# Batched VectorE exponentials and norm transposes by DMA in a one-core attention block

## The chip, the cores and the metric

The kernel runs on one core of a Trainium2 chip. The metric is the device time of one execution in microseconds, the median of several. A profile shows the span of one execution, which is some 2 us shorter than its time. Engines are named as in the profile: PE (matmul), PEld (weight load), DVE (VectorE), ACT (ScalarE), POOL (GpSimd), SP (SyncE). SP issues the DMAs.

## The reference

The block is a layer norm, an attention with 32 heads of 20 columns, and a gated product without activation, both with residuals, over 2048 tokens of 640 columns in bf16.

```python
def _A_ref(x, wqkv, wo):                       # B, S, D, H = 1, 2048, 640, 32; Dh = 20
    q, k, v = split(x @ wqkv)
    scores = einsum("bhqd,bhkd->bhqk", q, k) * Dh ** -0.5
    p = softmax(scores)
    return merge(einsum("bhqk,bhkd->bhqd", p, v)) @ wo

def _B_ref(x, w_gate, w_up, w_down):           # F = 1728
    return ((x @ w_gate) * (x @ w_up)) @ w_down

h  = x + _A_ref(layernorm(x), A_wqkv, A_wo)
h2 = h + _B_ref(layernorm(h), B_w_gate, B_w_up, B_w_down)
```

## The kernel before

The 2048 x 2048 scores of 32 heads need 134 million exponentials. They are handed out as 2048 PSUM banks of 128 x 512; four banks, one for each head of a group of four, make a slot. 313 of the banks go to VectorE, which makes the exponential from integer arithmetic, the rest to ScalarE. The queries are processed in six passes (512, 512, 384, 256, 256, 128 wide). The second stage (output projection, norm, gate, up, down) of a pass lies beside the attention of the next; the last one's is the tail.

The order of the instructions on each engine is fixed when the program is built: a list scheduler with a rough model of durations takes, on each engine and on the DMA queue, the ready task of the lowest priority number, and writes it down. On the chip each engine then runs its list in that order.

```python
def pick(self, eng):
    ...
    start = max(self.free[eng], best_r)
    ...
    t = min((t for r, t in ready if r <= start), key=lambda t: (t.prio, t.seq))
    return start, t
```

VectorE's exponentials take one pass per bank to add a bias, and then four passes over a pair of banks:

```python
def tail(self):                                # when two banks are collected
    ...
    def p2():
        nc.vector.tensor_scalar(f[:, 0:n, :], it[:, 0:n, :], 127, None, ALU.bitwise_and)
    def p3():
        nc.vector.tensor_scalar(h[:, 0:n, :], f[:, 0:n, :], QR, QK, ALU.subtract, ALU.mult)
    def p4():
        nc.vector.tensor_tensor(fb[:, 0:n, :], h[:, 0:n, :], f[:, 0:n, :], ALU.mult)
    def p5():
        nc.vector.tensor_tensor(e16[:, 0:n, :], it[:, 0:n, :], fb[:, 0:n, :], ALU.add)
    ...
```

The layer norm's rows are turned by PE in column tiles, and a copy takes them out of PSUM:

```python
def transpose_group(src, ev, dst, done, eng, prio, tag):
    def step(c):
        def fn(ps, first, last):
            pt = ps.bitcast(BF16)
            for i in range(4):
                nc.tensor.transpose(pt[32 * i:32 * i + 32, c * P:(c + 1) * P],
                                    src[:, c * P + 32 * i:c * P + 32 * i + 32], ident[:])
        return fn
    ...
```

All DMAs share SP's one queue.

The softmax here doesn't subtract the row's maximum and nothing guards it: scores larger than these inputs give would overflow.

## Time and profile before

| | before |
|---|---|
| time, median of 3 | 885.79 us (883.98 to 886.77) |
| span of the profiled run | 883.0 us |
| first exponential on ScalarE starts | 17.70 us |
| its last exponential ends | 834.8 us |
| tail: from there to the end | 48.2 us |
| ScalarE in exponentials (page) | 795.4 us in 758 instructions |
| ScalarE idle ahead of exponentials in between | 19.8 us: 14.3 before 210 us, 0.9 to 780, 4.6 after |
| VectorE busy | 754.5 us, 85% |

Read it as a sum along ScalarE: start, exponentials, idle, its few copies with the waits around them and the idle times too short for a bracket, tail: 17.7 + 795.4 + 19.8 + 1.9 + 48.2 = 883.0. The prediction's idle of 21.1 is counted by stretches and contains copies; the 19.8 here are the idle times that the timeline puts ahead of exponentials.

### The profile page before, as it was taken

How to read it: one execution, taken by the hardware profiler on the slowest of the kernel's cores; microseconds unless marked ns; L12 is line 12 of the kernel's file. 1: busy time of each engine (PE TensorE's matmuls, PEld its weight loads, DVE VectorE, ACT ScalarE, POOL GpSimd, SP SyncE). 2: the span in 40 equal slices, each digit the busy share in tenths (PEclk: the TensorE clock that was granted, in tenths of full speed). 3: DMA queues.
4: the chain of work that ended last, by engine and by line, in shares of the span. 5: the costliest groups of instructions: out<-in, count | busy, mean ns of one | idle time of the engine just before them, and what ended most of it. 6: DMA issues, size and time to landing. Idle time of an engine off the chain costs nothing. (4 is left out here: it accounts for less than half of the span.)

```text
span 883.0 us, 36981 instructions
## 1 busy us (share of the span) xinstructions
PE 832.6 (94%) x16596; PEld 367.6 (42%) x16596; DVE 754.5 (85%) x1608; ACT 804.4 (91%) x780; POOL 20.8 (2%) x32
## 2 busy tenths in 40 slices
PE   6999999999999999999999999999999999999995
PEld 2444342232334322222344433344444445565774
DVE  4654886999899999999999999989989997998652
ACT  3699989999999999999999999999999999998801
POOL 2020000000000000000000000000000000000000
PEclk9999999999999999999999999999999999999999
DMA  6131212212230233211310233161034311274100
GB/s 206 39 102 29 82 56 63 84 40 79 64 89 22 67 96 90 53 41 36 67 38 28 50 79 72 27 146 34 23 90 97 66 26 31 67 154 77 23 16 19
DMA packets 132950, 56.62 MB, mean 64 GB/s; under 512 B 103096, under 2 KB 130744, under 8 KB 132792
## 3 DMA queue, kind: packets, MB, share of 16 engines
q1 hardware_dynamic: 132792, 54.27, 24.5%
q8 instruction: 129, 2.11, 1.0%
q14 instruction: 29, 0.24, 0.1%
HBM read 45.89 MB, written 8.09 MB: 61 GB/s over the span
## 5 line engine op out<-in xcount | busy, mean ns | idle before, releaser
L740 ACT ACTIVATE E<-A 128x1536 bf16<-128x1536 f32 (+1 forms) x758 | 795.4, 1183 | 21.1 <-PE A L429 12.4
L429 PE MATMUL A<-qT,kT 32*128 32x256 bf16 (+3 forms) x3024 | 296.9, 299 | 22.8 <-ACT E L740 18.6
L429 PEld LDWEIGHTS <-kT 32*128 32x128 bf16 (+1 forms) x3768 | 101.5, 92 | 256.6 <-issue 216.0
L429 PE MATMUL acc<-E,Vx 128*32 128x256 bf16 (+3 forms) x2808 | 190.1, 304 | 4.7 <-ACT E L740 3.0
L754 DVE TENSOR_SCALAR i<-m 128x512 int16<-128x512 f32 x185 | 125.9, 684 | 11.8 <-PE m L429 10.5
L429 PEld LDWEIGHTS <-Vx 128*32 128x32 bf16 x3328 | 69.5, 95 | 102.5 <-issue 94.0
L784 DVE TENSOR_TENSOR fr<-hl,fr 128x1024 bf16<-128x1024 bf16 x157 | 107.0, 682 | 2.0
L787 DVE TENSOR_TENSOR ED<-i,fr 128x1024 int16<-128x1024 int16 x157 | 106.4, 678 | 1.3
L754 DVE TENSOR_SCALAR i<-A 128x512 int16<-128x512 f32 x128 | 87.7, 685 | 11.4 <-PE A L429 9.5
L429 PE MATMUL m<-lnT,Wr 128*32 128x512 bf16 (+7 forms) x1200 | 74.9, 347 | 2.2 <-DVE lnT L1016 0.8
L429 PE MATMUL m<-qT,kT 32*128 32x256 bf16 (+3 forms) x304 | 71.6, 297 | 0.0
L429 PE MATMUL m<-Wd,hh 128*32 128x320 bf16 (+1 forms) x1456 | 71.0, 301 | 0.2 <-DVE i L754 0.2
L429 PE MATMUL m<-ln2T,wg 128*32 128x512 bf16 (+2 forms) x980 | 70.0, 348 | 0.8 <-DVE i L754 0.8
L429 PE MATMUL m<-ln2T,wu 128*32 128x512 bf16 (+2 forms) x980 | 68.7, 348 | 1.3 <-DVE i L754 1.3
L429 PE MATMUL acc<-zt 128*32 128x512 bf16 (+3 forms) x992 | 67.2, 341 | 0.0
L781 DVE TENSOR_SCALAR hl<-fr 128x1024 bf16<-128x1024 int16 x157 | 65.4, 417 | 1.5
L778 DVE TENSOR_SCALAR fr<-i 128x1024 int16<-128x1024 int16 x157 | 64.4, 414 | 1.3
L429 PEld LDWEIGHTS <-hh 128*32 128x32 bf16 (+1 forms) x1792 | 42.9, 96 | 25.8 <-issue 16.4
L429 PE MATMUL m<-shared,On 128*32 128x320 bf16 x1024 | 49.0, 301 | 0.1
L1406 DVE TENSOR_TENSOR hh<-gs,m 128x512 bf16<-128x512 bf16 (+3 forms) x66 | 36.0, 545 | 9.4 <-PE m L429 5.0
L1395 DVE CAST gs<-m 128x512 bf16<-128x512 f32 (+5 forms) x62 | 35.1, 567 | 7.0 <-PE m L429 6.3
L429 PEld LDWEIGHTS <-Wr 128*32 128x32 bf16 (+1 forms) x1200 | 27.6, 96 | 27.2 <-issue 18.1
(71 smaller groups left out, 541.4 us busy)
## 6 DMA issues: line engine op xcount, KB each, us to landing
wg<-in_B_w_gate_dram SPq DMA_DIRECT2D x47, 160.0 KB
wu<-in_B_w_up_dram SPq DMA_DIRECT2D x47, 160.0 KB
rb<-rd SPq DMA_DIRECT2D x16, 256.0 KB
kT<-kq SPq DMA_DIRECT2D x24, 128.0 KB
kq<-stg SPq DMA_DIRECT2D x24, 120.0 KB
out_dram<-ot SPq DMA_DIRECT2D x16, 160.0 KB
shared<-in_A_x_dram SPq DMA_DIRECT2D x14, 160.0 KB
Wd<-in_B_w_down_dram SPq DMA_DIRECT2D x13, 160.0 KB
```

The costliest lines, as they stand in the source:

```text
L429: nc.tensor.matmul(out_, lhsT=lhsT, rhs=rhs, start=start, stop=stop)
L740: apart(readers, nc.scalar.activation(E[:, 0:size, :], src[:, 0:size, :], ACT.Exp, scale=LN2_ / UNIT))
L754: apart(readers, nc.vector.tensor_scalar(it[:, pos, :], bank.ap, BIAS, 0.0, ALU.add, ALU.max))
L778: nc.vector.tensor_scalar(f[:, 0:n, :], it[:, 0:n, :], 127, None, ALU.bitwise_and)
L781: nc.vector.tensor_scalar(h[:, 0:n, :], f[:, 0:n, :], QR, QK, ALU.subtract, ALU.mult)
L784: nc.vector.tensor_tensor(fb[:, 0:n, :], h[:, 0:n, :], f[:, 0:n, :], ALU.mult)
L787: nc.vector.tensor_tensor(e16[:, 0:n, :], it[:, 0:n, :], fb[:, 0:n, :], ALU.add)
L1395: r = en.add("DVE", dve_ns(w), [e, was], lambda: nc.vector.tensor_copy(gs[0:M, 0:w], ps[0:M, 0:w]), 1)
L1406: r = en.add("DVE", dve_ns(w), [e, ce, was], lambda: nc.vector.tensor_tensor(hh[0:M, 0:w], gs[0:M, 0:w], ps[0:M, 0:w], ALU.mult), 1)
```

## The change

It does four things. VectorE's batch becomes a whole slot of four banks. Layer norm rows are turned by DMA transposes instead of PE: all of the second stage, and tokens 1024 to 2047 of the first (`TURN = 2` of four chunks). In the tail, when the attention is done, matmuls use the full width of PE, and the last two head groups of the last pass and the last one of the pass before get their softmax sums by a small matmul instead of a round trip of three DMAs. The first weights that are loaded serve two head groups, and priorities and spreading of the second stage are set per pass. Two smaller settings change with these: VectorE may take banks from bank 96 on, and a limit at bank 1800 replaces a limit on the second stage's lateness (`LAG`).

```diff
+QK0 = 2 * HP * DH + PADR
+TURN = 2
+FAST_LAST = 2
+FAST_PREV = 1
+LNP = (1.2, 1.2, 1.2, 1.2, 0, 0)
+WP = (1, 1, 1, 1, 0, 0)
...
-SPREAD = 1.2
+SPREAD = (1.0, 1.0, 0.9, 0.8)
-LAG = 100
+M_END = 1800
...
-    I16t = tiles(keep, NI16, [P, 2, QW], I16, "i16_")
-    FR = tiles(keep, 2, [P, 2, QW], I16, "fr")
-    HL = tiles(keep, 1, [P, 2, QW], BF16, "hl")
-    ED = tiles(keep, NED, [P, 2, QW], I16, "ED")
+    DT = tiles(keep, ND, [P, HP, QW], I16, "D")
+    FR = keep.tile([P, HP, QW], I16, name="fr")
+    HL = keep.tile([P, HP, QW], BF16, name="hl")
...
     def columns(ps, lhsT, rhs, start, stop, n, width=P):
+        if pe.mode == "F":
+            mm(ps[0:width, 0:n], lhsT[:, 0:width], rhs, start, stop)
+            return
...
+        if g >= G - FAST.get(p, 0):
+            spread(p, g, free, a, b, spots)
+            return free
...
+    def turn_rows(src, dst, deps, prio):
+        return dma(lambda: nc.sync.dma_start_transpose(dst, src), deps, prio=prio, size=2 * P * D * 2)
...
+            if ch >= TURN:
+                lnT_ev[tt] = turn_rows(outs[i], lnT[:, :, tt * P:(tt + 1) * P], [evs[i]], 0)
+                ln_free[i] = lnT_ev[tt]
+                continue
...
-                g = transpose_group(l2[i % 2], e, ln2T[:, :, i * P:(i + 1) * P], done, "DVE", 1, f"t{p}{i}")
+                lev[i] = turn_rows(l2[i % 2][:], ln2T[:, :, i * P:(i + 1) * P], [e, fr.get("ln2T")], 0.5)
...
-D_START = 2 * HP * NT
+D_START = 96
```

## The prediction

> **What bounds the kernel now.** I read the page of the kernel before, then the busy time of each engine by stretches, then ScalarE in order of time, then the chain of work that ended last. The stretches cut the 883.0 us span into a start, the attention proper and a tail. Columns: stretch, length, then busy us (instruction count) of PE, weight load, VectorE, ScalarE, GpSimd, then granted clock, DMA share, GB/s.
>
> ```profile
> 1.70:17.70 16.00, 12.05 (x164) 5.24 (x165) 10.02 (x35) 3.84 (x7) 5.14 (x11) 1.00 0.96 284
> 17.70:34.70 17.00, 15.34 (x288) 7.03 (x291) 6.18 (x18) 8.57 (x9) 1.01 (x1) 1.00 0.16 47
> 34.70:57.40 22.70, 22.25 (x388) 8.50 (x384) 16.54 (x51) 22.11 (x24) 6.27 (x3) 1.00 0.16 46
> 57.40:89.10 31.70, 31.34 (x702) 14.18 (x694) 13.07 (x32) 29.48 (x32) 0.11 (x1) 1.00 0.24 60
> 89.10:200.00 110.90, 104.97 (x1537) 37.22 (x1535) 96.46 (x187) 106.93 (x101) 0.00 (x0) 1.00 0.22 66
> 200.00:800.00 600.00, 577.26 (x11035) 243.38 (x11035) 564.19 (x1160) 596.47 (x565) 5.94 (x7) 1.00 0.27 64
> 800.00:836.00 36.00, 33.41 (x1136) 22.26 (x1133) 28.01 (x73) 32.42 (x30) 0.70 (x1) 1.00 0.25 48
> 836.00:883.00 47.00, 36.03 (x1376) 29.82 (x1364) 20.04 (x57) 3.72 (x14) 0.55 (x1) 0.98 0.06 17
> ```
>
> From 200 to 800 us ScalarE is idle for 3.5 us of 600: it is the bound there. VectorE is at 94% and PE at 96%, but PE's share contains matmuls of zeros (acc<-zt and m<-zt) that only fill waits, so PE has room. ScalarE's first exponential starts at 17.70 and its last ends at 834.8. Between them it idles 11.2 us up to 89.1 (71.4 minus 8.57, 22.11 and 29.48), 4.0 up to 200, 3.5 up to 800 and 2.4 after: 21.1 us in all. Then follow 1.2 us to the last attention matmul at 836.0, and a tail of 47.0 us without exponentials, which hangs on PE: over 5% of the span. So the time is: start 17.7 + exponentials 795.4 (page) + ScalarE's idle and one copy 21.7 + 48.2. VectorE's busy time is in no term of it.
>
> The tail must be read in the chain that ended last (start, us, what). Its second half is:
>
> ```profile
> 864.40 0.40 PE b L429 x14
> 864.80 0.56 PE m L429 x40
> 865.36 1.01 PE b L429 x74
> 866.37 1.51 issue
> 867.87 0.85 PE b L429 x46
> 868.72 0.28 PE m L429 x20
> 869.00 0.28 PE b L429 x20
> 869.28 0.28 PE m L429 x20
> 869.56 0.29 PE b L429 x22
> 869.84 1.51 issue
> ```
>
> PE runs 14+40+74 = 128 matmuls, waits 1.51 us for nothing that the profile shows, runs 46+20+20+20+22 = 128, and waits 1.51 us again. A matmul and its weight load are two instructions, so the pause comes every 256. The page gives 129 instruction packets of 2.11 MB, 16.4 KB each. I take the pauses for PE waiting for its instructions: 128 pairs last 1.83 us there, so one block takes some 3.34 us to arrive (my estimate, the sum of both).
>
> **What the Trainium skill says.** "Runtime: NRT & Kernel Launch", section "Instruction fetch mechanics", says that instructions come in blocks of 16 KiB, 256 each, the refill mostly hidden. Size and period agree with this trace; "hidden" does not hold in the tail. "TensorE: Matmul & The Clock Gate", section "Back-to-back issue gap", gives about 81 ns per matmul for streams of load and matmul with 128 columns. Here 20 column-tiled matmuls, five full-width steps, take 0.28 us, 56 ns a step; no full-width step can be read in this trace, so it stays open which holds after the change. "VectorE: DVE Perf Modes", section "The perf-mode tier table", has bf16 tensor_scalar at four elements a cycle and tensor_tensor at two, 693 and 1224 ns for 2048. The trace has 418 and 683 ns for 1024, whose slopes lead to about those figures. "DMA: Bandwidth & Descriptors", section "DMA Transpose (X-bar)", tells only that the crossbar does transposes issued from SP or ACT for 2-byte types; no run here shows the duration yet.
>
> **The change part by part.**
>
> *Exponentials on VectorE.* Four rows of the groups view carry this (count | busy us, mean ns | idle):
>
> ```profile
> L784 DVE TENSOR_TENSOR fr<-hl,fr 128x1024 bf16<-128x1024 bf16 x156 | 106.6, 683 | 2.0
> L787 DVE TENSOR_TENSOR ED<-i,fr 128x1024 int16<-128x1024 int16 x156 | 106.0, 679 | 1.2
> L781 DVE TENSOR_SCALAR hl<-fr 128x1024 bf16<-128x1024 int16 x156 | 65.1, 418 | 1.5
> L778 DVE TENSOR_SCALAR fr<-i 128x1024 int16<-128x1024 int16 x156 | 64.1, 415 | 1.3
> ```
>
> A pair of banks costs 2195 ns, two pairs 4390. The forms of 512 columns take 424 and 288 ns, so each further 512 costs 258 and 128; at 2048 I get 1197 and 672 ns, 3738 for the four operations. By the instruction order there are 77 such batches and 3 of three banks instead of 156 pairs and one single: VectorE saves about 47 us. But banks on VectorE only rise from 313 to 317 of 2048, since the share of 0.17 stays. ScalarE goes from 539 two-bank and 219 three-bank exponentials to 528 and 225. In the saturated stretch 32 two-bank ones take 29.48 us, 921 ns each; with 424 ns more for a third bank (the means by form are 1485 and 1061 ns) the 758 add to 795.4 at 927 and 1351 ns. The new mix is 528 x 0.927 + 225 x 1.351 = 793.4 us: 2 us saved. The 47 us of VectorE lie beside ScalarE and buy almost nothing. Starting those banks at 96 rather than 256, and taking fewer after 1800, moves them without adding any.
>
> *Transposes by DMA.* 16 of the second stage and 8 of the first leave PE (20 matmuls, about 0.45 us each, 11 us) and VectorE (0.48 us each, 11.6 us). Off the bound again, but in the first stage the keys of tokens 1024 on now wait for four transposes on the one queue. In PE's new order only two units of scores stand before 140 value matmuls, one dense and one direct projection and 16 zero matmuls, some 6 us of PE against 1.9 us of ScalarE: I expect a new ScalarE gap of 4 to 5 us there, more if the transposes are slow.
>
> *The start.* ScalarE lacks work here:
>
> ```profile
> 29.31 0.59 ACT L1154 CAST kT<-m 128x512 bf16<-128x512 f32 x1 [0.73 <-PE m L429]
> 34.72 22.11 ACT L740 ACTIVATE E<-A 128x1024 bf16<-128x1024 f32 x24 [4.83 <-PE A L429]
> ```
>
> Group 1's projections come late behind values and transposes. The change loads 172 weight columns first, enough for both groups, and PE's order now has group 1 before the values. That should remove most of the 8 us idle of 17.7 to 34.7, and start the first exponential about 1 us later (16 more matmuls, four steps at 0.43 us, in part hidden). With the new gap and 2 us less idle after 89, ScalarE's idle should fall by about 6, net of the start 5 us.
>
> *The tail.* After the last attention matmul the new order has 76 full-width steps of 256 columns (before: 108), 56 + 28 of 320 in the down projections, 16 in the output projection and 140 of 128. At 0.109, 0.136 and 0.056 us: 8.3 + 11.4 + 2.2 + 7.8 = 29.7 us; before, the same count gives 33.7 with the transpose, plus 4.3 us from the last projection to the end and some 9 of pauses, which is the 47. Full-width matmuls need a quarter of the instructions: 128 pairs of 128 columns then last 7.2 us, above the 3.34 of a block, so the pauses (1.04, 1.57, 1.51, 1.51, 0.80) go. The last pass's sums no longer go through three DMAs: the quotient needs copy, one matmul, a reciprocal of about 0.94 us (slope of the reciprocal rows, 6.25 ns an element) and a product, some 2.2 us instead of the 13 from the copy at 836.08 to the quotient at 849.4. So its output projection and norm lie beside the older pass's work, and a DMA transpose there has some 9 us of cover. Adding 4.3 us and 2 us of small waits, the tail is 36 us at 56 ns a step, 39.5 at 81; I take 37: 10 us saved.
>
> *Sum.* 885.8 - 2 - 5 - 10 = 868.8, so 869 us.
>
> **The rivals.** First, VectorE is the true bound (94% busy), and 47 + 11.6 us less of it brings 30 us or more, about 850. For it speaks PE's waiting on line 754; against it ScalarE's 3.5 us idle in 600. Second, DMA transposes are slow and block the one queue: PE waits in order, the new gap in the start grows to 10 or 15 us and the gain shrinks to 880. For it: eight transposes in the busiest part of the start; against: they have slack behind tokens 0 to 1023, and only chunks 2 and 3 use them. Third, full-width steps pay for weight loads and the tail saves only 7 us: 872. Fourth, longer VectorE operations (1.2 us instead of 0.68, not interruptible) hold PSUM banks and cost ScalarE 3 to 5 us: 873.
>
> **Range and chances.** The tail is counted best (7 to 11.5 us), the start is worst (between a loss of 4 and a gain of 9), VectorE's relief gives 0 to 5. Together 860 to 878. The 2% line is at 868.1, just under the point. Faster by over 2%: 0.45; within: 0.52; slower by over 2%: 0.03.
>
> **What will show it.** ScalarE's exponentials at 793 us and its idle near 15; VectorE at about 700 us busy; the tail from the last attention matmul at 37 us without 1.5 us issue pauses; ScalarE's gap near 30 us gone and one near the keys of token 1024. I am wrong if ScalarE stops being the bound between 200 and 800, if a transpose takes over 5 us to land, or if the tail stays over 42 us.

## More of the kernel before

Heads have 20 columns, but the scores' operands are laid out in strips of 32 rows. Keys and queries of head groups 2 and later reach this layout through a buffer in device memory (`kq`): a projection is staged and written there (`kq<-stg`), and read back in strips (`kT<-kq`, `qT<-kq`). The rows between are zeros, written once.

```python
e_pad0 = None
for h in range(0, H - DENSE0, 8):
    for c in range(4):
        def pad(h=h, c=c):
            ...                                # kq[0] rows 20..31 of 8 heads <- zt
        e_pad0 = dma(pad, [e_zt, e_pad0], size=8 * 12 * QW * 2, prio=1.5)
```

Twelve such writes, each waiting for the one before, at the last priority; a read of `qT<-kq` waits for all of them.

## The result, and the profile after

| | before | after |
|---|---|---|
| time, median of 4 of the same rounds | 885.91 us | 890.35 us (888.42 to 891.75) |
| span | 883.0 | 888.2 |
| first exponential starts | 17.70 | 17.27 |
| ScalarE in exponentials | 795.4 (758) | 794.5 (753) |
| ScalarE idle ahead of them: before 210 us / to 780 / after | 14.3 / 0.9 / 4.6 | 26.7 / 4.8 / 7.7 |
| last exponential ends | 834.8 | 852.0 |
| tail | 48.2 | 36.2 |
| VectorE busy | 754.5 | 723.8 |

The ratio is 1.0052, with a 95% interval of 1.0027 to 1.0077. Every ratio here is the mean time of one kernel's fast runs over that of the other's of the same rounds, so not quite the ratio of the medians that are quoted. The change is half a per cent slower, where a gain of 2% was predicted, and lies outside the predicted range.

The stretches of the changed kernel, cut at its own gaps. Columns as in the prediction: stretch, length, then busy us (count) of PE, weight load, VectorE, ScalarE, GpSimd, then granted clock, DMA share, GB/s.

```profile
17.27:34.70 17.43, 16.30 (x344) 7.58 (x342) 7.06 (x20) 16.01 (x18) 1.01 (x1) 1.00 0.19 56
34.70:57.40 22.70, 21.28 (x428) 9.90 (x428) 16.60 (x54) 14.84 (x17) 5.77 (x3) 1.00 0.42 76
...
86.50:102.50 16.00, 12.76 (x272) 7.88 (x271) 6.84 (x15) 0.02 (x1) 0.00 (x0) 0.89 0.38 103
200.00:800.00 600.00, 575.75 (x10640) 239.33 (x10641) 537.52 (x885) 594.62 (x562) 7.13 (x7) 1.00 0.28 66
852.00:888.20 36.20, 32.39 (x345) 24.75 (x344) 16.79 (x49) 3.70 (x14) 0.55 (x1) 0.97 0.07 19
```

Up to 34.7 us ScalarE is now busy for 16.0 of 17.4 us: the start is better, as predicted. Then it loses 7.9 us in the second stretch, and from 86.5 to 102.5 us it does nothing at all, while PE is busy for 12.8 of these 16 us. From 200 to 800 it is idle for 5.4 us instead of 3.5, although VectorE is busy for 27 us less. The tail is 36.2 us.

VectorE's batches in the view of groups (count | busy us, mean ns of one | idle before them):

```profile
L787 DVE TENSOR_TENSOR fr<-hl,fr 128x2048 bf16<-128x2048 bf16 x77 | 93.4, 1214 | 0.7
L781 DVE TENSOR_SCALAR fr<-D 128x2048 int16<-128x2048 int16 x77 | 52.8, 686 | 0.9
```

They cost 1214 and 686 ns against 1197 and 672 worked out, so that the sizes of the operations were right within some 2%. The table of the Trainium skill that the prediction names ("VectorE: DVE Perf Modes", section "The perf-mode tier table") agrees, with 1224 and 693 ns for 2048 elements.

The tail in the chain of work that ended last, at the place that answers to the one shown before:

```profile
871.92 0.66 PE b L438 x10
872.58 0.28 PE m L438 x5
872.86 0.84 PE b L438 x15
```

Columns are start, us, what. Five full-width steps of 128 columns take 0.28 us, 56 ns each (0.84 us for fifteen), and nothing stands between the lines. The chain has 120 such steps from 871.92 to 878.84 us, 58 ns each on average. In the changed kernel's chain from 852 us to the end no "issue" is longer than 0.12 us, where before there were four of over a microsecond.

So the loss lies in ScalarE's idle time. The timeline of ScalarE, first of the kernel after, then of the kernel before (start, us from there on, engine, line, operation, shapes, count, and in brackets the idle time ahead of it and who ended it):

```profile
56.79 29.73 ACT L748 ACTIVATE E<-A 128x1024 bf16<-128x1024 f32 x32 [6.62 <-PE A L438]
102.52 41.63 ACT L748 ACTIVATE E<-A 128x1536 bf16<-128x1536 f32 x39 [16.00 <-PE m L438]
```

```profile
89.11 31.13 ACT L740 ACTIVATE E<-A 128x1536 bf16<-128x1536 f32 x30 [2.21 <-PE m L429]
```

At the same point of the work, where the scores of the first two head groups are used up and those of group 2 must begin, ScalarE waited 2.21 us before and waits 16.00 us after. The chain of waits of the changed kernel into that gap:

```profile
90.21 6.76 DMA rb<-rd
...
96.99 0.69 DVE On L918
97.69 0.41 DVE Vx L1288
...
98.14 3.95 PE m L438 x51
```

VectorE stood at a product that needs the sums spread by a DMA (`rb<-rd`, 6.76 us from issue to landing). Behind the product in its order was the copy `Vx` that PE needed for a bank of PSUM, and PE then ran 51 column-tiled matmuls in 3.95 us. But this is the last part of the gap only. Why PE had nothing else to do is in the list of the DMA queue of the changed kernel (start, us, queue and line, kind, what, count):

```profile
41.69 5.31 SPq L1056 DMA_TRANSPOSE lnT<-shared  x4
...
51.18 4.69 SPq L1056 DMA_TRANSPOSE lnT<-shared  x3
...
65.20 0.68 SPq L1277 DMA_DIRECT2D kq<-zt  x1
75.56 0.33 SPq L1242 DMA_DIRECT2D kq<-stg  x1
...
90.79 0.69 SPq L1277 DMA_DIRECT2D kq<-zt  x1
...
93.56 0.38 SPq L1256 DMA_DIRECT2D qT<-kq  x1
```

and of the kernel before:

```profile
61.23 2.02 SPq L1228 DMA_DIRECT2D kq<-zt  x3
78.72 0.35 SPq L1193 DMA_DIRECT2D kq<-stg  x1
...
81.92 0.48 SPq L1207 DMA_DIRECT2D qT<-kq  x1
```

The queries of group 2 are read (`qT<-kq`) at 93.56 us after the change and at 81.92 us before. They wait for the last of the twelve zero rows (`kq<-zt`). In the kernel before the last three go out at 61.23 us, ahead of a staged projection (`kq<-stg`) that is not ready before 78.72 us. In the changed kernel eight transposes take the queue between 41.69 and 55.87 us, 1.2 to 1.35 us each and one 2.08, and the zero rows, chained and at the last priority, are put behind them. When the queue reaches the staged projection that is not ready before 75.56 us, it stands idle for 9.7 us, and four zero rows are still behind it; the last goes out at 90.79 us. So, by this reading, the transposes made late something that has nothing to do with them. PE's list was built with the same lateness in it: between the last scores of group 1 and the next scores it is busy for 13.5 us, against 2.9 us at that place in the kernel before. So PE is busy in the gap with projections, and with zeros (48 of the 296 matmuls there).

This is a reading of one trace. It needed to be tested, since the gap has three candidates: the transposes themselves, the zero rows behind them, and the longer batches of VectorE.

### The profile page after: what moved, and what is told of

Read it like the earlier page. It is cut to its first block, busy times and chain, and to the rows that moved or that the text cites.

```text
span 888.2 us, 34459 instructions
## 1 busy us (share of the span) xinstructions
PE 837.5 (94%) x15481; PEld 367.3 (41%) x15481; DVE 723.8 (81%) x1280; ACT 803.3 (90%) x775; POOL 22.9 (3%) x35
## 4 chain that ended last, share of the span: by engine, by line
ACT 59%; PE 27%; DVE 7%; issue 5%; DMA 1%; SPq 0%; DVEq 0%; POOL 0%; ACTq 0%
ACT E L748 59%; PE m L438 12%; PE A L438 7%; PE acc L438 5%; PE b L438 3%; DVE D L766 2%; DMA rb<-rd 1%; DVE fr L787 1%; DVE fr L781 1%; DVE hl L784 1%; DVE st L1012 0%; DVE accS L902 0%; DVE D L790 0%; PE m L1040 0%; DVE Vx L1288 0%
## 5 line engine op out<-in xcount | busy, mean ns | idle before, releaser
L748 ACT ACTIVATE E<-A 128x1536 bf16<-128x1536 f32 (+1 forms) x753 | 794.5, 1194 | 40.3 <-PE A L438 21.0
L766 DVE TENSOR_SCALAR D<-m 128x512 int16<-128x512 f32 x197 | 134.2, 684 | 26.1 <-PE m L438 24.8
L787 DVE TENSOR_TENSOR fr<-hl,fr 128x2048 bf16<-128x2048 bf16 (+1 forms) x80 | 96.3, 1203 | 0.7
L790 DVE TENSOR_TENSOR D<-D,fr 128x2048 int16<-128x2048 int16 (+1 forms) x80 | 96.2, 1203 | 0.3
L766 DVE TENSOR_SCALAR D<-A 128x512 int16<-128x512 f32 x120 | 82.1, 684 | 13.7 <-PE A L438 12.2
L438 PE MATMUL acc<-zt 128*32 128x512 bf16 (+3 forms) x1192 | 85.0, 348 | 0.0
L781 DVE TENSOR_SCALAR fr<-D 128x2048 int16<-128x2048 int16 (+1 forms) x80 | 54.5, 681 | 1.0
L784 DVE TENSOR_SCALAR hl<-fr 128x2048 bf16<-128x2048 int16 (+1 forms) x80 | 54.4, 680 | 1.0
L438 PEld LDWEIGHTS <-hh 128*32 128x32 bf16 (+2 forms) x1540 | 42.4, 96 | 27.8 <-issue 16.8
L438 PEld LDWEIGHTS <-zt 128*32 128x32 bf16 x1324 | 32.7, 97 | 35.5 <-issue 24.3
L1439 DVE CAST gs<-m 128x512 bf16<-128x512 f32 (+2 forms) x65 | 36.5, 562 | 10.0 <-PE m L438 9.5
```

The costliest lines, as they stand in the source:

```text
L438: nc.tensor.matmul(out_, lhsT=lhsT, rhs=rhs, start=start, stop=stop)
L748: apart(readers, nc.scalar.activation(E[:, 0:size, :], src[:, 0:size, :], ACT.Exp, scale=LN2_ / UNIT))
L766: apart(readers, nc.vector.tensor_scalar(it[:, pos, :], bank.ap, BIAS, 0.0, ALU.add, ALU.max))
L781: nc.vector.tensor_scalar(FR[:, 0:n, :], it[:, 0:n, :], 127, None, ALU.bitwise_and)
L784: nc.vector.tensor_scalar(HL[:, 0:n, :], FR[:, 0:n, :], QR, QK, ALU.subtract, ALU.mult)
L787: nc.vector.tensor_tensor(fb[:, 0:n, :], HL[:, 0:n, :], FR[:, 0:n, :], ALU.mult)
```

## The experiments

Each run is shown against the kernel before of the same rounds. "Idle" is ScalarE's idle ahead of exponentials, before 210 us / to 780 / after. "Tail" is from the end of the last exponential to the end of the span. All sixteen gave a result within the tolerance.

| run | what | time, us | ratio, 95% | idle | tail |
|---|---|---|---|---|---|
| (the change) | | 890.35 | 1.0052 [1.0027, 1.0077] | 26.7 / 4.8 / 7.7 | 36.2 |
| e1_first_stage_on_pe | change, first-stage transposes on PE | 878.23 | 0.9941 [0.9909, 0.9974] | 14.1 / 5.0 / 4.1 | 39.4 |
| e6_zero_rows_early | change, zero rows early | 889.22 | 1.0053 [1.0023, 1.0083] | 14.1 / 4.2 / 9.7 | 43.0 |
| e7_early_and_pe | both | 872.65 | 0.9867 [0.9834, 0.9900] | 13.3 / 4.9 / 5.4 | 33.6 |
| b1_tail_alone | before, with the tail's part | 878.97 | 0.9938 [0.9904, 0.9973] | 12.3 / 0.9 / 7.1 | 38.5 |
| b2_slots_alone | before, with batches of four | 886.96 | 1.0051 [1.0018, 1.0084] | 15.3 / 1.8 / 9.7 | 47.3 |
| b5_tail_and_first_weights | b1 and wider first weights | 881.23 | 0.9979 [0.9957, 1.0000] | 13.2 / 4.9 / 5.2 | 39.8 |
| e8_no_dma_transposes | e7, second stage on PE too | 880.46 | 0.9973 [0.9950, 0.9997] | 13.2 / 6.8 / 6.0 | 37.1 |
| f5_more_on_vector | e7, more banks on VectorE | 890.26 | 1.0073 [1.0037, 1.0108] | 13.1 / 10.7 / 15.8 | 46.4 |
| d2_zero_rows_late | e1, zero rows held back | 886.77 | 1.0056 [1.0034, 1.0077] | 19.3 / 1.9 / 4.9 | 44.3 |
| a1_pairs_again | change, pairs on VectorE | 884.46 | 1.0030 [1.0001, 1.0058] | 26.1 / 3.6 / 3.2 | 36.2 |
| b7_tail_and_second_transposes | b1, second-stage transposes by DMA | 877.78 | 0.9946 [0.9920, 0.9973] | 13.3 / 5.4 / 2.9 | 42.1 |
| g1_best_of_parts | e7 with pairs | 874.16 | 0.9915 [0.9891, 0.9939] | 11.9 / 3.4 / 1.1 | 41.3 |
| h1_best_mended | g1, one dependence mended | 870.87 | 0.9846 [0.9817, 0.9875] | 11.9 / 3.4 / 0.9 | 38.5 |
| e7_again | e7 repeated | 873.55 | 0.9862 [0.9834, 0.9891] | 12.2 / 4.8 / 5.2 | 33.5 |
| h2_zero_rows_mended | e6, mended | 886.41 | 1.0003 [0.9964, 1.0041] | 17.2 / 4.2 / 9.4 | 38.7 |
| h4_first_stage_on_pe_mended | e1, mended | 878.38 | 0.9913 [0.9875, 0.9950] | 16.0 / 4.3 / 7.5 | 36.6 |

How far a single profile can be read: e1 and h4, e6 and h2, and the two runs of e7 have the same instructions in the same order on ScalarE, VectorE and SP, and the mend of the h runs acts on the second stage alone. Yet their idle before 210 us differs by 1.9, 3.1 and 1.1 us. Smaller differences in that column mean nothing.

One warning holds for seven of these kernels (e1, e6, f5, d2, b1, b7, g1). In their orders the rows of the last pass are turned into `ln2T` before the older pass's last gate or up group has read all of it, because the program makes the transposition wait for the last up group alone. A few matmuls then read the next pass's rows. The results still passed the comparison with the reference, but a small part of their values is not what it should be, and the matmuls wait for the transposition. The kernels before and after do not show this wait in their traces. The h runs mend it. (In b1 it is VectorE's copy into `ln2T` that comes too early.)

### Which part makes the gap

**The first stage's transposes back on PE.**

```diff
-TURN = 2
+TURN = 4
```

> The changed kernel with the first stage's eight DMA transposes put back on TensorE, all else as changed. Theory A (the transposes stand in the one in-order DMA queue ahead of the zero rows that the queries of head group 2 need, so the scores after the first 128 banks start late) and theory B (the transposes themselves are slow, keys come late) both expect the 16.0 us ScalarE gap at 86.5 us to shrink under 4 us and the 6.6 us gap at 50 us to shrink to under 4: about 890 - 12 - 3 = 875 us. Theory C (VectorE's four-bank batches or their earlier start at bank 96 hold PSUM banks and starve ScalarE) expects the gap to stay: 888 or more.

The longest idle of ScalarE is now 3.21 us, and the time falls by 1.1% of the kernel before: from 1.0052 to 0.9941. The gap at the keys of token 1024 falls to 2.70 us too:

```profile
53.56 29.65 ACT L748 ACTIVATE E<-A 128x1024 bf16<-128x1024 f32 x32 [2.70 <-PE A L438]
```

So eight transposes cost about 10 us, and the rest of the change is worth 0.6%. This does not yet tell whether the transposes or what stands behind them makes the gap.

**The zero rows early, the transposes kept.** The writes are unchained and get a priority ahead of other background transfers.

```diff
-    e_pad0 = None
+    e_pad0 = []
...
-            e_pad0 = dma(pad, [e_zt, e_pad0], size=8 * 12 * QW * 2, prio=1.5)
+            e_pad0.append(dma(pad, [e_zt], size=8 * 12 * QW * 2, prio=0.5))
+    e_pad0 = Max(e_pad0)
```

(The eight writes of `e_pad` likewise.)

> The changed kernel, DMA transposes kept, but the twenty zero-row writes are no longer chained one behind another and go first in the DMA queue. Theory A: the 16.0 us gap falls below 5 us although all transposes stay on DMA, time about 878 us. Theory B (slow transposes): gap and time stay near 890. Theory C: the same, 890.

The 16 us gap is gone with all transposes still on the queue. ScalarE's two largest idles are these:

```profile
53.35 52.71 ACT L748 ACTIVATE E<-A 128x1024 bf16<-128x1024 f32 x54 [4.10 <-PE A L438]
111.10 6.03 ACT L748 ACTIVATE E<-A 128x1024 bf16<-128x1024 f32 x6 [5.04 <-PE A L438]
```

Its last exponential ends at 841.2 us instead of 852.0, as it should. But the 878 us of Theory A are missed, the time stays at 889.22 us: the tail is 43.0 instead of 36.2 us, and ScalarE idles 9.7 us late. The early gap was given back at the end. One part of that is the wait described above; what the mended run makes of it follows below.

**Both.**

> Both: zero rows early and the first stage's transposes on TensorE. If both causes are separate and add up, about 3 us under the better of the other two, some 872 us, and ScalarE's idle up to 200 us under 10 us. If zero rows alone were it, no better than with zero rows early alone.

The edit is that of the two runs above. At 872.65 us, 0.9867, it beats both the kernel before and the change, with early idle of 13.3 us (not under 10, as expected) and a tail of 33.6 us.

**The zero rows late, without any first-stage transpose.** If their lateness is the cause, it must make the gap without help.

```diff
-            e_pad0 = dma(pad, [e_zt, e_pad0], size=8 * 12 * QW * 2, prio=1.5)
+            e_pad0 = dma(pad, [e_zt, e_pad0, Later(lambda: lnT_ev.get(8))], size=8 * 12 * QW * 2, prio=1.5)
```

This is e1 with the zero rows of the queries held until the first tile of tokens from 1024 on is turned.

> The changed kernel with the first stage's transposes on TensorE (no DMA transpose there), but the twelve zero-row writes for the queries held back until the first row of chunk 2 is turned. Theory A (late zero rows make the gap, whatever delays them): a ScalarE gap of 10 us or more near bank 128 (about 86 us) is back, time 8 to 12 us over the same kernel with zero rows as they were (878). Rival (the transposes on the queue, or VectorE's batches, make the gap): no gap over 4 us there, time as 878.

```profile
96.46 114.00 ACT L748 ACTIVATE E<-A 128x1536 bf16<-128x1536 f32 x108 [15.00 <-PE m L438]
```

The gap is back with 15.00 us, at the same point of the work, in a kernel whose first-stage rows are turned by PE. With e6 this settles what makes the gap: the transposes alone do not, the late zero rows alone do. The runs line up by the start of the last zero row's write, the read of group 2's queries, and ScalarE's idle at bank 128:

| run | last zero row, us | `qT<-kq`, us | idle at bank 128, us |
|---|---|---|---|
| before | 62.63 | 81.92 | 2.21 |
| e6 | 45.68 | 57.13 | none |
| e1 | 72.67 | 76.36 | 1.87 |
| d2 | 85.18 | 91.09 | 15.00 |
| the change | 90.79 | 93.56 | 16.00 |

**Pairs on VectorE again, the rest of the change kept.** The hunks of the batches are taken back, from `NED = 4` to `self.pair = []`.

```diff
-ND = 3
+NED = 4
+NI16 = 3
...
+            if len(self.pair) == 2:
+                self.tail()
```

> The changed kernel with VectorE's batches back to pairs, all else as changed. If the batches cost what they cost alone (0.5%): 4 to 5 us faster, about 886, and the 16 us gap near 86 us stays, since its cause is the queue. If the batches caused the gap, it shrinks under 4 us and the time falls to about 875.

```profile
102.11 47.30 ACT L754 ACTIVATE E<-A 128x1536 bf16<-128x1536 f32 x44 [15.83 <-PE m L440]
```

The gap does not move, so the batches are not its cause. Nor is their earlier start: in the changed kernel the first bank on VectorE is taken at 102.5 us, when the gap ends. The ratio is 1.0030 with pairs and 1.0052 with slots, the intervals overlap.

### What each other part is worth

**The tail's part on the kernel before:** full-width matmuls when attention is done, and the sums of the last head groups spread by a matmul.

```diff
+FAST_LAST = 2
+FAST_PREV = 1
...
+        if g >= G - FAST.get(p, 0):
+            spread(p, g, free, a, b, spots)
+            return free
...
+        if pe.mode == "F":
+            mm(ps[0:width, 0:n], lhsT[:, 0:width], rhs, start, stop)
+            return
```

> The kernel before with only the tail's parts of the change (full-width matmuls after the last attention matmul, the last quotients by a matmul and a reciprocal on chip), transposes all on TensorE. The tail of 48 us (last exponential to end) should become 37 to 38 us with no 1.5 us pauses: 885.9 - 10 = 876 us. If the gain in the tail came from other parts (second-stage work drawn forward, DMA transposes), it stays above 882.

The tail goes from 48.2 to 38.5 us, by 9.7, but the time only by 0.6%, some 5.5 us, where 10 were expected. Against the profile of the kernel before, 1.7 us are lost in exponentials and 0.6 in idle (2.5 more near the end, 2.0 less early); the span falls by 7.9, more than the mean of the runs does.

**The batches of four alone, on the kernel before.**

```diff
-NED = 4
-NI16 = 3
+ND = 3
...
-            if len(self.pair) == 2:
-                self.tail()
```

> The kernel before with only VectorE's batches changed from two banks to a whole slot of four (three tiles of a slot instead of three plus four of a pair); start at bank 256, transposes and tail as before. Theory A (batches free VectorE beside ScalarE and buy nothing, ScalarE has 544 and 213 exponentials for 539 and 219): VectorE's four tail operations fall from 343 to about 296 us busy, time within 0.5% of before. Rival (longer, uninterruptible VectorE operations hold banks): 0.5 to 1.5% slower, more ScalarE idle between 90 and 800 us. Rival (VectorE was the bound): 2% or more faster.

VectorE's busy time falls by 19 us, from 754.5 to 735.1, and the time does not fall: 1.0051, with ScalarE's late idle at 9.7 us instead of 4.6. Relief of VectorE buys nothing, and in this form it costs a little.

**The wider first weights, on top of the tail's part.**

```diff
+QK0 = 2 * HP * DH + PADR
...
-    e_qk0 = [None, load_w(D, D + 160)]
-    e_qk0[0] = load_w(0, 160)
+    e_qk0 = [None, load_w(D, D + QK0)]
+    e_qk0[0] = load_w(0, QK0)
...
-        ws = ([e_k, e_qk0[1]] if b == 1 else [e_q, e_qk0[0]]) if g == 1 else [e_qk0[b]]
+        ws = [e_qk0[b]]
```

> The kernel before with the tail's parts and the wider first weight load (group 1's projections before the values), nothing else: pairs, TensorE transposes, start at bank 256. If the start gains of the changed kernel (7.5 us less ScalarE idle before 35 us) and of the tail (about 10 us) stand alone and add: 4 to 5 us under the tail alone, some 0.985 of before. If the list schedule gives the start's gain back later: no better than the tail alone, 0.994.

From 17.2 to 35 us ScalarE is busy for 15.55 us instead of 11.46 in b1, but from 35 to 60 us for 20.94 instead of 24.41: of 4.1 us gained, 3.5 are lost at the next supply of scores. PE is busy for 40.6 of these 42.8 us in b5 and 40.3 in b1, but 6.9 and 4.5 of them are matmuls of zeros, so that it is not shown that PE had no room to be ahead. The whole is not faster than b1 (0.9979 against 0.9938).

**The second stage's transposes.** First taken away from the good kernel e7, that is, all transposes on PE, then added to b1.

```diff
-                lev[i] = turn_rows(l2[i % 2][:], ln2T[:, :, i * P:(i + 1) * P], [e, fr.get("ln2T")], 0.5)
+                g = transpose_group(l2[i % 2], e, ln2T[:, :, i * P:(i + 1) * P], done, "DVE", 1, f"t{p}{i}")
```

> The kernel with zero rows early and first-stage transposes on TensorE, now with the second stage's sixteen transposes on TensorE too, so no DMA transpose is left. Theory A (second-stage transposes are hidden either way): within 0.4% of the same kernel with them by DMA (872.65 us in the rounds before). Rival (PE and VectorE work saved there, 7 us each, counts in the last stage): 3 to 5 us slower.

Without them the ratio is 0.9973, where e7 had 0.9867 (0.9862 when it was repeated). The span grows by 6.5 us, 3.5 of them in the tail and 2.3 in idle. The second stage's transposes by DMA are a gain here of about 1%, more than both forecasts had. In the tail it is work that was left over: PE is busy for 33.2 us in e8's tail and for 29.8 in e7's.

The reverse edit on b1:

> The kernel before with the tail's parts and the second stage's transposes by DMA, nothing else: pairs, start and first stage as before. If the second-stage DMA transposes bring in this company what they brought above (0.9%), 0.985 of before, 870; if they only shifted the list schedule there, 0.994 as the tail alone.

Here they bring nothing (0.9946 against 0.9938): the exponentials end 1.9 us earlier, but the tail grows from 38.5 to 42.1 us, and 2.67 us of it are the wait for the transposition that the warning tells of. This one was not run mended.

**More banks on VectorE,** on e7.

```diff
-M_END = 1800
+M_END = 2048
...
-SHARE = 0.17
+SHARE = 0.19
...
-D_LOAD = 4000.0
+D_LOAD = 6000.0
```

> The kernel with zero rows early and first-stage transposes on TensorE, with the share of banks for VectorE raised to 0.19, its load limit raised and the limit at bank 1800 lifted: 346 banks on VectorE instead of 320. If VectorE's freed time is spendable, ScalarE's exponentials fall by about 11 us and the time to about 865. If the last stage is bound by PSUM banks and PE instead, ScalarE idles more after 780 us and the time stays at 872 or rises.

VectorE gets 346 banks, where e7 has 319 by the count of its exponentials. ScalarE's whole busy time falls from 804.7 to 792.9 us, but its idle rises from 23.6 to 39.5 us, and the tail to 46.4. It is 2% slower than e7. In the middle of the attention, from 210 to 780 us, idle doubles from 4.9 to 10.7. ScalarE is the bound only as long as PE and VectorE keep it supplied; there is little slack on either.

**Pairs in the good kernel.** The edit of a1 on e7.

> Zero rows early, first-stage transposes on TensorE, second-stage by DMA, the tail, and VectorE in pairs. If slots cost 0.5% here too: about 868, 0.982 of before, and the best so far. If slots are neutral in this company: 872 as with them.

ScalarE's idle is 16.4 us, the lowest so far, and the exponentials end at 829.3 us, 9 us earlier than in e7. But the tail is 41.3 us, and the gain is not seen. The chain of waits has the reason in it:

```profile
842.44 0.34 PE b L440 x3
842.78 0.02 issue
842.80 2.67 DMA ln2T<-l
```

PE does three matmuls of a group, and then waits 2.67 us for the transposition of the last pass's rows before the other two.

### The dependence behind the transposition

By then the open point was why the tails with full-width matmuls were 33.6 to 46.4 us long. The mend makes the transposition wait for every gate and up group of the older pass. It changes no instruction's place, only which waits for which.

```diff
-                ups.append(gu.ev)
-            fr["ln2T"] = ups[-1]
+                ups += [gg.ev, gu.ev]
+            fr["ln2T"] = Max(ups)
```

> The best-of-parts kernel with one dependence mended: its DMA transpose into ln2T now also waits for the last gate group, not only the last up group, so two matmuls no longer stand behind it (2.67 us in the chain of the run before). If that wait was on the path: tail from the last exponential's end 41.3 -> about 38.6, ratio to before about 0.9915 - 2.7/882.5 = 0.9885, some 871.5 us. Rival: the same 2.7 us of transfer comes back as a wait of the last pass's own first step, tail stays at 41, ratio 0.9915.

In the mended kernel the chain has no such wait at that place:

```profile
842.27 6.88 PE b L440 x47
```

The tail goes from 41.3 to 38.5 us, by about the 2.67 us of the transfer. At 870.87 us, 0.9846, this is the fastest kernel, and the early overwrite of `ln2T` is gone from its order.

> The kernel with zero rows early and the first stage's transposes on PE, batches of four banks, once more, beside the mended one on the same chip. If its 0.9867 was a fair measurement: 0.985 to 0.989 again, tail 33 to 35, span about 872. Its order has no matmul behind the transposition, so the mend changes no instruction of it (checked). Rival: it was a lucky sample and returns at 0.99 or over, equal to or slower than the mended pairs.

0.9862 after 0.9867: e7's gain was real, its tail is 33.5 us again. The mended kernel with pairs is as fast within the intervals. What it gains in the attention (exponentials end at 829.1 against 837.9 us) it pays in the tail, where more of the older pass's second stage is left over: PE is busy for 34.7 us there, in e7's tail for 29.8, and the tails differ by the same 4.9 or 5.0 us. This holds for the other tails too. Without a wait for the transposition, the tail is PE's busy time in it and 3.8 to 4.2 us more (the change, a1, e7, e8, h1, h2, h4), with the wait 6.5 to 6.9 more (e1, e6, f5, d2, b7, g1); in b1 and b5 it is 4.5 and 5.0 more, and with the column-tiled matmuls and pauses of the kernel before 11.0.

> The run with the zero rows early (ratio 1.0053) with the same dependence mended. If the 2.67 us were on the path: ratio about 1.002, tail 43.0 -> about 40.3. If the tail's length comes from how much older second-stage work is left over (33.4 us counted), the tail stays over 40 all the same, and the rest of its loss against the kernel before is ScalarE's late idle (9.7 us).

The tail falls from 43.0 to 38.7 us, more than the 2.67 that were expected, and the ratio from 1.0053 to 1.0003, within intervals that touch. Idle was higher by 2.8 us in this profile, so that of 4.3 us in the tail little is left in the span (884.2 to 883.8). With the early gap gone and the tail mended, the transposes of the first stage still leave this kernel 1.4% behind e7. The tail is 5.2 us longer because 4.9 us more of PE's work are left over for it. What makes up the rest, and why more is left over, is not settled: 9.4 us of late idle against 5.2, and 17.2 of early idle against 12.2, of which some 3 are the scatter of one profile, are spread over many places.

> The run with the first stage's transposes back on PE (ratio 0.9941) with the same dependence mended: ratio about 0.991, 875.5 us, tail 39.4 -> 36.7. If it does not move, the wait only traded places with another one in the tail, and the differences between the tails come from somewhere else.

The tail falls from 39.4 to 36.6 us, as it should, and the ratio from 0.9941 to 0.9913, less than the intervals can tell apart.

## Why the prediction was wrong

**The bound (right).** ScalarE was taken as the bound and VectorE's saving as worth almost nothing. Batches of four alone were not faster but 0.5% slower, and with more banks on VectorE the time grew. The exponentials fell by 0.9 us where 2 were worked out. The first rival, VectorE as the true bound with a gain of 30 us, is refuted. VectorE's relief, which has no weight in the sum, was itself set too high: its busy time fell from 754.5 to 723.8 us, by 30.7, where 47 and 11.6 were counted and 700 us expected. The prediction multiplied mean durations, and these overlap: the 1608 instructions on VectorE in the kernel before last 851 us when added up (my sum over the trace) in 754.5 us of busy time, 60 ns for each. The durations of the four operations fell by 42 us (343 to 301), their share of the busy time only by 25 (307 to 282). The fourth rival, that the longer operations cost ScalarE 3 to 5 us, is not refuted: all three comparisons (the change against a1, the kernel before against b2, e7 against h1 in the same rounds) lean that way by 0.2 to 0.5%, though in the first and the last the intervals overlap. Only g1, which has the wait for the transposition, is slower with pairs than e7.

**The tail (right).** Predicted from the last attention matmul: 47 to 37 us, 10 saved. Measured from the last exponential, where the old one is 48.2: 36.2 us, 12.0 saved. The part alone gave 9.7. PE's busy time in the tail fell from 37.2 to 32.4 us, and what is not PE's work from 11.0 to 3.8. The open question of 56 or 81 ns per full-width step was decided by the five steps in 0.28 us. The pauses of 1.5 us are gone, as the count of instructions said. Two readings of the prediction are wrong and change nothing in it: 128 pairs take 1.97 us in the lines that it shows (864.40 to 866.37), not 1.83, so that a block would take 3.48 us; and VectorE's banks began at bank 128 in the kernel before, not at 256, as some of the expectations say too.

**The start (right in its place, wrong in what it is worth).** The idle near 30 us went, and ScalarE is busy for 16.0 of the first 17.4 us. The first exponential starts 0.4 us earlier, not 1 us later. But b5 shows that the gain moved the wait instead of removing it: the same scores end sooner, and the next ones, which do not come earlier, are waited for. The gap expected at the keys of token 1024 came with 6.6 us instead of 4 to 5.

**The step that failed** is this one: "ScalarE's idle should fall by about 6, net of the start 5 us." The idle rose by 19.4 us, from 19.8 to 39.2. The sum along ScalarE is then, from before to after: start -0.4, exponentials -0.9, idle +19.4, copies -0.9, tail -12.0, together +5.2 us, which is what the spans differ by. Of the rise, 13.8 us are the gap at head group 2 (2.21 to 16.00), and 6.0 the one at the keys of token 1024 (0.59 to 6.62). The prediction did name the channel, as its second rival: "DMA transposes are slow and block the one queue", with a gap of 10 or 15 us and a time of 880. It was set aside because the transposes had slack behind tokens 0 to 1023. That looked at the transposes' own consumers. The transposes were not slow either: 1.2 to 1.35 us of the queue (one 2.08), and 2.67 us from issue to landing in the late chains, under the 5 us named as the limit. What was not looked at is who stood behind them in the queue, whose order is fixed when the program is built: the zero rows, chained, at the last priority, needed by the queries of group 2. e6 and d2 show this from both sides.

That is shown for the gap, and not for all of the lost time. Without the gap (e6) the ratio stayed at 1.0053, and with the tail mended as well (h2) it is 1.0003; the transposes have to leave the first stage (e7, 0.9862) to win the other 1.4%. What they cost there beside the gap is open.

**A term that was set too low:** the second stage's transposes were booked as "off the bound again". In e7 against e8 they are worth about 1%, 6.5 us of span, of which 3.5 lie in the tail. These 3.5 are the 3.4 us by which PE is busy longer in e8's tail. By the prediction's own rate PE saves 16 times 0.45 us, 7.2 us, in all; that this is why less is left over when the tail begins is argued, not shown. On b1 the same edit brought nothing.

**What stays open.** The late idle of ScalarE moves between 0.9 and 15.8 us from kernel to kernel, and no run isolates its cause. The settings that no run isolates (the bank where VectorE starts, the limit at bank 1800, `SPREAD`, `LNP`, `WP`) may have a part in every comparison of the change, or a kernel built on it, with the kernel before. Every edit reorders all lists, so a part of each difference belongs to the new order and not to the part that was edited.

## What to carry to other kernels

Before moving work to a DMA queue that runs in order, read the queue's new list and ask for each entry behind the new ones who needs it and when; what has slack of its own may still make something unrelated late. Where the order of all engines is built from one list of priorities, small transfers that everything later depends on must not be at the last priority, and one change alone is measured with the reordering that it causes. A gain at one place of a chain of supply is worth only what the next place can use.

## What the Trainium skill lacked or had wrong

- "TensorE: Matmul & The Clock Gate", section "Back-to-back issue gap": its 81 ns per pair of load and matmul with 128 columns does not hold here. Five full-width steps took 0.28 us, 56 ns each, and 120 of them 58 ns each; this is the section's figure for an isolated matmul, about 56 ns, which it calls too low for such a stream.
- "Runtime: NRT & Kernel Launch", section "Instruction fetch mechanics": the refill is called mostly hidden. In the tail of the kernel before PE paused four times for 1.04 to 1.57 us, the last three times 256 instructions apart, and with a quarter of the instructions the pauses were gone. No run changed the instruction count alone, so the cause rests on their period and their disappearance.
- "DMA: Bandwidth & Descriptors", section "DMA Transpose (X-bar)", gives no time for a transpose that a kernel could be planned with; another table of the page has a bandwidth alone. Here one of 128 x 640 bf16 elements mostly took 1.2 to 1.5 us of the issuing queue (2.1 to 2.2 us for three of the changed kernel's 24), and 2.67 us from issue to landing.
- "DMA: Bandwidth & Descriptors", section "Queues, rings and completion order", tells how the engines behind a queue take turns, not what an entry at the issuing engine that waits for its data does to those behind it; "Perfetto Trace Analysis" draws the wait of such an entry, but not the cost for the entries behind. Here one such entry held the queue for 9.7 us, with four unrelated writes behind it.
